# Planned page places, stored transform parts and shifted due times in a one-core FNet and feed-forward kernel

## The chip, the cores and the metric

The kernel runs on one core of a Trainium2 chip. The metric is the device time of one execution in microseconds (us); three runs of the kernel before gave 699.50, 700.13 and 700.16, median 700.13. The engines of the core are named as the profile names them: PE multiplies matrices (PEld is its weight load), DVE is the vector engine, ACT the scalar engine, POOL is GpSimd, and SP only issues DMAs here. Each engine works through its own queue in order; POOL and SP also issue DMAs from theirs.

## The reference

The input `x` has 2048 rows (tokens) of 512. All arrays are float32.

```python
a = jnp.einsum("bsd,ed->bse", x, dft_hid_re)        # x: after layernorm
b = jnp.einsum("bsd,ed->bse", x, dft_hid_im)
y = jnp.einsum("ts,bse->bte", dft_seq_re, a) - jnp.einsum("ts,bse->bte", dft_seq_im, b)

h = x + _A_ref(_layernorm(x, axis=-1), ...)         # _A_ref gives y
h2 = h + W2(silu(W1(_layernorm(h, axis=-1))))       # 512 -> 1792 -> 512
```

So there is a layernorm, a transform along the sequence and along the model dimension of which the real part is kept, a residual sum, a second layernorm and a feed-forward block with SiLU.

## The kernel before

**Precision.** Every float32 operand is split in a rounded part ("hi", type fp32r, made by ACT) and a remainder ("lo", made by DVE). A product is three matmuls: hi by hi, hi by lo, lo by hi (`three`, L124). The two halves of such a split are put in the order of work by `halves` (L87): ACT a lead of 2.2 us (`GAP_US`) ahead of DVE, and DVE with a lead of `PREP_US` = 8 us ahead of the matmuls in most places.

**Stages.** The sequence transform comes first, over four blocks (`c` is real or imaginary part, `q` is a half of the tokens): `plain(0,0)` multiplies directly; `fast(1,0)`, `fast(0,1)` and `fast(1,1)` use seven products for eight (Strassen's scheme in Winograd's form), for which DVE makes sums of blocks of the matrix (`prep`, L426, with four raw blocks loaded by `load`, L421). After two blocks of one `q` follows `mix(q)` (L486), the transform along the model dimension: four products per half `tau`, with the matrix `hid` loaded and split in hi and lo (`load_hid`, `round_h`) in `tau` = 0 and kept for `tau` = 1, once for each `q`. Then `norm_h(q, tau)` (L534) makes the second layernorm of a quarter of the tokens. The order on PE is plain(0,0), fast(1,0), mix(0), fast(0,1), fast(1,1), mix(1), up(0), down(0), up(1), down(1); `up` (W1 and SiLU) and `down` (W2) use seven products for eight as well, and the first products of `down` are put ahead of the last two of `up`.

**norm_h in steps.** `mean` and `var` each add on DVE and then add over partitions on POOL (`total`, L526, an all-reduce). `row` writes one row of 512 variances to HBM, `gather` reads it back as 128 x 4, `root` and `finish` compute the inverse root on DVE, `finish` also issues its write to HBM, `spread` reads it back to all partitions (tile `r`), `scale` (L577) multiplies on DVE. All these DMAs are in POOL's queue. For `q` = 0 `store` writes the normalized parts to HBM (`nd`), from which `load_hn` reads them later; for `q` = 1 they stay on chip until `up(1)`.

**Weights.** `sums_w1` (L622) makes sums of blocks of W1, splits them and stores hi and lo to HBM (`sd`); `fetch_w1` (L648) reads them back for each `q` and loads the plain blocks too. `make_w2` (L751) does the same for W2 (`wd`, four stores of 512 KB for each of seven groups `p`), and `fetch_w2` reads them. These jobs stand beside other stages, at starts that are written out by hand in L908 and L915.

**Order of the work.** Nothing is issued in the order of the source. Each stage puts its pieces in a list `events` with a due time (L130 to L144). The clock of this list counts matmuls alone, 0.2265 us each, from the first one. By it plain(0,0) ends at 87.0, fast(1,0) at 163.1, mix(0) at 206.6, fast(0,1) at 282.7, fast(1,1) at 358.8, mix(1) at 402.3, and the first part of `down(0)` ends at 497.4. A piece that is to stand ahead of a matmul step has a lead: 18 us for a load (`LOAD_US`), 8 for a split. The list is sorted by due time (L940), and the order in which the pieces then come is the order of each engine's queue. In the profile the first matmul starts at 7.25 us, so due time t is at about t + 8.7 in the span in the first part, and later where PE has been idle meanwhile. These due times are called "planned" below.

**Pages.** All tiles of 4 KB per partition are "pages" out of one pool of 51 (L62, L68). Places go round: the 52nd page takes the place of the first, the 53rd that of the second, and so on. Whoever writes a page first waits until the last reader or writer of the tile that had the place is done.

**up and its copies.** In `up`, `post` (L689) copies bank Y out of PSUM to the pages `cp` and `cq` on ACT (n = 1, 6, 5), DVE adds the other bank to it into the page `g` (n = 2, 5, 4), and ACT applies SiLU in place. Before a `down` that finishes later, `keep_bank` (L817) copies PSUM banks out on ACT; `post123` does so for banks 1, 2 and 3 together after the step with n = 3 of the last group. `sums_g` (L799) and two splits prepare each group for the second part of `down`; they start at `first` = clock - 13 and follow every 5 us (L884). `up(q, lead, ...)` spreads the seven sums and splits of its moving operand (`sums_h`, `round_t`, L712) over `lead` us ahead of it: 62 for q = 0, 70 for q = 1.

Of the kernel before, what the change touches and what calls it, by code (L numbers as in the profile page):

```python
# [7 lines left out]
F32 = mybir.dt.float32  # L8
BF16 = mybir.dt.bfloat16
F32R = mybir.dt.float32r  # L10
# [21 lines left out]
PREP_US = 8.0  # L32
LOAD_US = 18.0
GAP_US = 2.2
ORDERED = (mybir.EngineType.PE, mybir.EngineType.DVE, mybir.EngineType.Activation, mybir.EngineType.Pool)


@with_exitstack
def fnet_ffn_kernel(
# [7 lines left out]
    out: bass.AP,  # L47
):


# [19 lines left out]

# [295 lines left out]
    def fast(c, q):  # L366
# [50 lines left out]
        for jj in range(NJ):  # L417
            key = {n: ("A", c, q, n, jj) for n in (5, 7, 6, 4)}
            B4 = {}

            def load(jj=jj, B4=B4):  # L421
                for k, tau in ((0, 1), (0, 0), (1, 1), (1, 0)):
                    load_seq(c, q, jj, k, tau, ("B", k, tau))
                    B4[k, tau] = raw.pop(("B", k, tau))

            def prep(n, jj=jj, B4=B4, key=key):  # L426
                b11, b12, b21, b22 = (B4[k] for k in ((0, 0), (0, 1), (1, 0), (1, 1)))
                o, a, b = {5: (b11, b12, b11), 7: (b12, b22, b12), 6: (b22, b22, b11), 4: (b21, b22, b21)}[n]
                sub(o, a, b)
                raw[key[n]] = o  # L430

            for n in (5, 7, 6, 4):
# [6 lines left out]
                def post(n=n):  # L439
# [9 lines left out]
                    else:  # L449
# [36 lines left out]
    def mix(q):  # L486
        for tau in range(2):
            for c in range(2):
                for i in range(2):
# [34 lines left out]
    nd = dram.tile([2, 2, P, 2, 512], F32, name="nd")  # L524

# [8 lines left out]
    def norm_h(q, tau, start):  # L534
# [22 lines left out]
        def row():  # L557
            nc.gpsimd.dma_start(token[0], ln.pop("v")[0:1, 1, :])

# [13 lines left out]
        def spread():  # L573
            ln["r"] = page(f"r{q}{tau}")
            nc.gpsimd.dma_start(ln["r"][:, 0, :], token[1].partition_broadcast(P))

        def scale(e):  # L577
            v = ln.pop(e)
            for n in range(2):
                nc.vector.tensor_tensor(v[:, n, :], v[:, n, :], ln["r"][:, 0, :], op=ALU.mult)  # L580
            hn[q, e, tau] = v

        def store():
            for e in range(2):
                nc.gpsimd.dma_start(nd[tau, e], hn.pop((q, e, tau)))
# [11 lines left out]
    def load_hn(k, tau):  # L597
        t = hn[0, k, tau] = page(f"hn{k}{tau}")
        nc.sync.dma_start(t, nd[tau, k])

# [47 lines left out]
    def fetch_w1(q, p):  # L648
        load_w1(("W1", q, p), p, False)
# [4 lines left out]
        W[q, p] = {5: (sh, sl, 0), 6: (sh, sl, 1), 7: (sh, sl, 2), 3: (sh, sl, 3)}  # L654

    def round_w1(q, p):
        r = raw.pop(("W1", q, p))
        ah, al = (page(f"w{n}{q}{p}", F32R, (4, 256)) for n in ("ah", "al"))
        nc.scalar.activation(ah[:, 1:, :], r[:, 1:, :], AF.Copy)
        W[q, p].update({1: (ah, al, 1), 2: (ah, al, 2), 4: (ah, al, 3)})  # L660
        return lambda: rest([(al[:, 1:, :], r[:, 1:, :], ah[:, 1:, :])])

    def up(q, lead, between):

        bank, cp = {}, {}

# [18 lines left out]

        def add(f, tau, src, other):
            nc.vector.tensor_tensor(g[q, f][:, tau, :], src, other, op=ALU.add)  # L687

        def post(n, p):  # L689
            if n == 1:  # L690
                cp[p, 0] = page(f"cp{q}{p}")
                cp[p, 1] = page(f"cq{q}{p}")
                for i in range(2):
                    g[q, 2 * p + i] = page(f"g{q}{p}{i}")
                nc.scalar.activation(cp[p, 0][:, 0, :], bank[p, "Y"], AF.Copy)
            elif n == 2:
                add(2 * p, 0, bank[p, "X"], cp[p, 0][:, 0, :])
            elif n == 6:
                nc.scalar.activation(cp[p, 0][:, 1, :], bank[p, "Y"], AF.Copy)
            elif n == 5:  # L700
                nc.scalar.activation(cp[p, 1][:, 0, :], bank[p, "Y"], AF.Copy)
                add(2 * p + 1, 1, bank[p, "V"], cp[p, 1][:, 0, :])
            elif n == 3:
                silu(2 * p, 1, bank[p, "Y"])
            elif n == 4:
                add(2 * p + 1, 0, bank[p, "V"], cp[p, 0][:, 1, :])
# [12 lines left out]
        for v in order:  # L719
# [5 lines left out]
            if n == 1:  # L725
                before = [(LOAD_US, lambda p=p: fetch_w1(q, p)), *halves(PREP_US, lambda p=p: round_w1(q, p))]
            after = [(0, lambda n=n, p=p: post(n, p))]
# [23 lines left out]
    def make_w2(start, p):  # L751
# [6 lines left out]
        def store():  # L758
            for n, t in enumerate((*kept["U"], *kept["V"])):
                nc.gpsimd.dma_start(wd[p, n], t.bitcast(F32))  # L760
# [14 lines left out]
    def down(q, later):  # L775
# [108 lines left out]
        first = clock[0] - PREP_US - 5  # L884
        for p in range(NP):
# [7 lines left out]
        for n, p in order:  # L893
            before, after = [], []
            if n == 6:
                before.append((LOAD_US, lambda p=p: fetch_w2(p, V, 2)))
            if n == 6 and p in (2, 3) and not later:
# [19 lines left out]
    for k in range(2):  # L917
        for tau in range(2):
            at(clock[0] - 80 + 2 * k + tau, lambda k=k, tau=tau: load_hn(k, tau))
# [17 lines left out]


    traced, last = nc.cur_bb.bb.instructions, {}
    for *_, f in sorted(events, key=lambda v: v[:3]):  # L940
        n = len(traced)
        with ExitStack() as order:
            for ins in last.values():
                order.enter_context(tc.issue_after(ins))
            f()
        for ins in traced[n:]:
            if ins.engine in ORDERED:
                last[ins.engine] = ins

# [33 lines left out]
```

## Time and profile before

| | |
|---|---|
| median of three runs | 700.13 us (699.50 to 700.16) |
| the profiled execution's own time | 696.92 us |
| its span, from the first to the last instruction | 694.8 us |
| PE busy | 680.4 us, 98%, 2965 matmuls (13 of them to warm up) |
| DVE busy | 557.6 us, 80% |
| ACT busy | 337.9 us, 49% |
| POOL busy | 80.0 us, 12% |
| DMA | 170.70 MB, 246 GB/s over the span |
| granted TensorE clock | 0.996 |

A matmul's record is 0.39 us long though a new one starts every 0.23 us, since they overlap; so the busy share of PE says that it seldom has nothing to do, and the loss of time is better read from the distance between starts, or from the number of matmuls in slices of equal length.

### The profile page before, as it was taken

Reading aid. Unit: us, or ns where it says so; the run is one execution under the profiler, and the core shown is the slowest. Engines: PE = TensorE matmul, PEld = TensorE weight load, DVE = VectorE, ACT = ScalarE, POOL = GpSimd, SP = SyncE. Lnnn points to the kernel's source line nnn. Section 1 sums busy time; section 2 is a strip of 40 time slices with the busy share of each in tenths; the row PEclk is TensorE's granted clock in tenths of the full one; section 3 lists DMA queues with packets and bytes.
Section 4 is the critical chain, followed back from the end, with each engine's and each line's share of the span. In section 5 each row is a group of like instructions: output and inputs, shape, how many; then the busy total and the mean of one; then the engine's idle time right before and its main releaser. Section 6 shows DMA issues by size and latency. Waiting matters only on the chain.

```text
span 694.8 us, 8384 instructions
## 1 busy us (share of the span) xinstructions
PE 680.4 (98%) x2965; PEld 555.9 (80%) x2965; DVE 557.6 (80%) x715; ACT 337.9 (49%) x421; POOL 80.0 (12%) x99
## 2 busy tenths in 40 slices
PE   8999999999999999999999999989989999999997
PEld 5788888888888887888888888877868888888885
DVE  6599896997887998998998977848999336449975
ACT  4655785544343533555461425637754354565420
POOL 1021020000035211020010232211000000000000
PEclk9999999999999999999999999999999999999999
DMA  8855879677787576899995454578745646688332
GB/s 316 301 194 183 313 258 412 230 259 231 229 282 253 200 260 200 302 319 391 415 386 173 161 193 148 164 267 336 264 168 189 214 145 242 234 325 304 135 139 91
DMA packets 55993, 170.70 MB, mean 246 GB/s; under 512 B 6288, under 2 KB 13456, under 8 KB 55952
## 3 DMA queue, kind: packets, MB, share of 16 engines
q1 hardware_dynamic: 46320, 136.60, 56.5%
q0 software_dynamic: 9632, 33.58, 12.6%
q8 instruction: 23, 0.38, 0.2%
q14 instruction: 18, 0.15, 0.1%
HBM read 133.44 MB, written 36.72 MB: 245 GB/s over the span
## 4 chain that ended last, share of the span: by engine, by line
PE 79%; DVE 7%; issue 5%; DMA 5%; POOL 2%; ACT 2%; DVEq 0%; POOLq 0%
PE m L127 9%; PE m L128 9%; PE m L126 9%; PE y L126 6%; PE y L128 6%; PE y L127 6%; PE f L126 6%; PE f L128 6%; PE f L127 6%; PE c L126 3%; PE c L127 3%; PE c L128 3%; DMA r<-tk 2%; PE vx L128 2%; PE vx L126 2%
## 5 line engine op out<-in xcount | busy, mean ns | idle before, releaser
L77 ACT ACTIVATE ph<-raw 128x1024 fp32r<-128x1024 f32 x98 | 101.7, 1057 | 91.3 <-DVE raw L415 56.5
L81 DVE TENSOR_TENSOR pl<-raw,ph 128x1024 fp32r<-128x1024 f32 x98 | 118.6, 1220 | 16.5 <-ACT ph L77 10.0
L127 PE MATMUL m<-pl,S 128*128 128x512 f32 x192 | 74.9, 390 | 1.6 <-DVE pl L81 1.6
L128 PE MATMUL m<-ph,S 128*128 128x512 f32 x192 | 74.7, 389 | 0.0
L126 PE MATMUL m<-ph,S 128*128 128x512 f32 x192 | 74.7, 389 | 0.0
L126 PE MATMUL f<-gth,wf 128*128 128x512 f32 x168 | 66.1, 393 | 2.7 <-ACT p L819 2.7
L127 PE MATMUL f<-gtl,wf 128*128 128x512 f32 x168 | 66.1, 393 | 0.0
L128 PE MATMUL f<-gth,wf 128*128 128x512 f32 x168 | 66.1, 393 | 0.0
L77 ACT ACTIVATE gth<-g 128x1024 fp32r<-128x1024 f32 x42 | 43.9, 1055 | 41.3 <-DVE g L803 30.9
L415 DVE TENSOR_TENSOR raw<-raw,raw 128x1024 f32<-128x1024 f32 x48 | 60.6, 1263 | 2.1 <-DMA raw<-in_seq 2.1
L126 PE MATMUL m<-ph,X 128*128 128x512 f32 x144 | 56.0, 389 | 0.0
L127 PE MATMUL m<-pl,X 128*128 128x512 f32 x144 | 56.0, 389 | 0.0
L128 PE MATMUL m<-ph,X 128*128 128x512 f32 x144 | 56.0, 389 | 0.0
L81 DVE TENSOR_TENSOR gtl<-g,gth 128x1024 fp32r<-128x1024 f32 x42 | 50.3, 1219 | 0.2 <-DMA wd<-Ul 0.2
L687 DVE TENSOR_TENSOR g<-vx,cp 128x512 f32<-128x512 f32 x28 | 19.3, 689 | 33.0 <-PE vx L128 19.3
L127 PEld LDWEIGHTS m<-pl,S 128*128 128x128 f32 x192 | 36.0, 188 | 9.9 <-DVE pl L81 2.5
L127 PE MATMUL c<-pl,X 128*128 128x512 f32 x112 | 43.5, 390 | 0.0
L126 PE MATMUL c<-ph,X 128*128 128x512 f32 x112 | 43.3, 391 | 0.2 <-ACT X L217 0.2
L128 PE MATMUL c<-ph,X 128*128 128x512 f32 x112 | 43.4, 389 | 0.0
L126 PEld LDWEIGHTS m<-ph,S 128*128 128x128 f32 x192 | 36.1, 188 | 7.5
L128 PEld LDWEIGHTS m<-ph,S 128*128 128x128 f32 x192 | 36.0, 188 | 7.4
L126 PEld LDWEIGHTS f<-gth,wf 128*128 128x128 f32 x168 | 32.0, 190 | 10.1 <-ACT p L819 3.2
(259 smaller groups left out, 1479.8 us busy)
## 6 DMA issues: line engine op xcount, KB each, us to landing
raw<-in_seq SPq DMA_DIRECT2D x98, 512.0 KB, 5.7
wf<-wd SPq DMA_DIRECT2D x56, 512.0 KB, 5.4
sf<-sd SPq DMA_DIRECT2D x28, 512.0 KB, 6.1
w<-in_ffn SPq DMA_DIRECT2D x28, 256.0 KB, 4.5
hid<-in_hid SPq DMA_DIRECT2D x8, 512.0 KB, 6.9
c<-cd SPq DMA_DIRECT2D x8, 512.0 KB, 5.7
h<-in_xT SPq DMA_DIRECT2D x8, 512.0 KB, 5.1
hd<-h POOLq DMA_DIRECT2D x8, 512.0 KB, 4.0
```

The lines of the kernel that those rows point to most:

```text
L77: nc.scalar.activation(hi, src, AF.Copy, scale=sign)
L81: nc.vector.tensor_tensor(lo, src, hi, op=ALU.subtract)
L126: nc.tensor.matmul(acc, wh, mh, start=first, stop=False, skip_group_check=on)
L127: nc.tensor.matmul(acc, wh, ml, start=False, stop=False, skip_group_check=on)
L128: nc.tensor.matmul(acc, wl, mh, start=False, stop=last, skip_group_check=on)
L415: nc.vector.tensor_tensor(o, a, b, op=ALU.subtract)
L687: nc.vector.tensor_tensor(g[q, f][:, tau, :], src, other, op=ALU.add)
```

## The change

- **Pages.** The pool has 51 places with a name each instead of a round. The whole event list is run once ahead of time with stand-ins (`Stub`) that only note, in order, which page each operation uses and at which planned time. `Plan.places` then gives each new page, among the places whose former tile has had all its uses in that order, the one that by the plan has been free for longest; a use counts as over 4 us after its planned time for a matmul, 10 us for a DMA and 2 us for others.
- **The transform's split parts.** In `mix(0)` hi and lo of `hid` are also stored to HBM (`store_hid`, eight DMAs of 512 KB in POOL's queue); in `mix(1)` eight DMAs of 512 KB in SP's queue (`fetch_hid`, lead 13) take the place of four loads and four splits.
- **Second layernorm.** `norm_h(0,1)` starts 57 us after the end of `mix(0)` instead of 6. Its steps have other offsets, for q = 1 `root` and what follows are some 6 us (`scale` 12) later. `spread` writes into the page `v`, and `r` is gone. Both `q` go through HBM (`nd`), and `up` loads them 18 us ahead of its splits.
- **up and down.** The lead of `up(1)` is 24 instead of 70. `cp` and `cq` are gone: ACT copies into the page `g`, and DVE adds in place. `keep_bank` of banks 1 and 2 comes one step (6 matmuls) earlier, and `sums_g` starts 4 us earlier. Stored weights are fetched with a lead of 13 instead of 18.
- **Weights' sums.** Other starts for `sums_w1` and `make_w2`; among them the groups p = 2, 3, 4 of `make_w2` go from planned 291, 311, 331 (in `fast(1,1)`) to 369, 395, 411 (in `mix(1)` and the start of `up(0)`).
- **fast.** The four raw blocks are not loaded together, but two for n = 5, one for n = 7 and one for n = 4, each 18 us ahead of its step.

```diff
+FETCH_US = 13.0
+FREE_US = {None: 2.0, "matmul": 4.0, "dma_start": 10.0}
...
+class Plan:
+    def __init__(self):
+        self.now, self.uses, self.taken, self.last = 0.0, 0, [], []
+    def page(self, name, dt=F32, shape=(2, 512)):
+        self.taken.append(self.uses)
+        self.last.append((self.uses, self.now))
+        return Stub(self, len(self.taken) - 1)
+    def used(self, page, op):
+        self.uses += 1
+        self.last[page] = self.uses, self.now + FREE_US.get(op, FREE_US[None])
+    def places(self):
+        free = [(-1, -1000.0 + n) for n in range(PAGES)]
+        for taken, last in zip(self.taken, self.last):
+            n = min((n for n in range(PAGES) if free[n][0] <= taken), key=lambda n: free[n][1])
+            free[n] = last
+            yield n
...
-    pages = ctx.enter_context(tc.tile_pool(name="pages", bufs=PAGES))
+    pages = ctx.enter_context(tc.tile_pool(name="pages", bufs=1))
...
-        return pages.tile([P, *shape], dt, tag="pg", name=name)
+        return pages.tile([P, *shape], dt, tag=f"pg{next(places)}", name=name)
...
-            def load(jj=jj, B4=B4):
-                for k, tau in ((0, 1), (0, 0), (1, 1), (1, 0)):
+            def load(n, jj=jj, B4=B4):
+                for k, tau in {5: ((0, 1), (0, 0)), 7: ((1, 1),), 4: ((1, 0),)}[n]:
...
-                step(12, mm, before + [(LOAD_US, load)] * (n == 5), [(0, post)] if jj == NJ - 1 and n in (6, 4) else ())
+                step(12, mm, before + [(LOAD_US, lambda n=n, load=load: load(n))] * (n != 6), [(0, post)] if jj == NJ - 1 and n in (6, 4) else ())
...
+    hs = dram.tile([2, 2, 2, P, 2, 512], F32, name="hs")
+    def store_hid(c, i):
+        for n, t in enumerate(H[c, i]):
+            nc.gpsimd.dma_start(hs[c, i, n], t.bitcast(F32))
+    def fetch_hid(c, i):
+        t = [page(f"H{c}{i}{n}") for n in range(2)]
+        for n in range(2):
+            nc.sync.dma_start(t[n], hs[c, i, n])
+        H[c, i] = [v.bitcast(F32R) for v in t]
...
-                    if tau == 0:
-                        before = [(LOAD_US, lambda c=c, i=i: load_hid(c, i)), *halves(PREP_US, round_h)] + before
+                    if tau == 0 and q == 0:
+                        before = [(LOAD_US, lambda c=c, i=i: load_hid(c, i)), *halves(PREP_US, round_h),
+                                  (PREP_US - 4, lambda c=c, i=i: store_hid(c, i))] + before
+                    elif tau == 0:
+                        before.append((FETCH_US, lambda c=c, i=i: fetch_hid(c, i)))
...
-            norm_h(q, tau, clock[0] + 2 + 4 * tau)
+            norm_h(q, tau, clock[0] + (57 if q == 0 and tau else 2 + 4 * tau))
...
-            ln["r"] = page(f"r{q}{tau}")
-            nc.gpsimd.dma_start(ln["r"][:, 0, :], token[1].partition_broadcast(P))
+            nc.gpsimd.dma_start(ln["v"][:, 0, :], token[1].partition_broadcast(P))
...
-        for d, f in ((0, mean), (7, lambda: center(0)), (9, lambda: center(1)),
-                     (10, lambda: square(0)), (12, lambda: square(1)), (15, var), (21, row), (24.5, gather),
-                     (30, root), (32.5, finish), (36, spread), (43, lambda: scale(0)), (45, lambda: scale(1))):
+        late = 6 * q
+        for d, f in ((0, mean), (8, lambda: center(0)), (10, lambda: center(1)),
+                     (11, lambda: square(0)), (13, lambda: square(1)), (16, var), (22, row), (25.5, gather),
+                     (31 + late, root), (33.5 + late, finish), (36.5 + late, spread),
+                     (45 + 2 * late, lambda: scale(0)), (47 + 2 * late, lambda: scale(1))):
             at(start + d, f)
-        if q == 0:
-            at(start + 47, store)
+        at(start + 49 + 2 * late, store)
...
             if n == 1:
-                cp[p, 0] = page(f"cp{q}{p}")
-                cp[p, 1] = page(f"cq{q}{p}")
                 for i in range(2):
                     g[q, 2 * p + i] = page(f"g{q}{p}{i}")
-                nc.scalar.activation(cp[p, 0][:, 0, :], bank[p, "Y"], AF.Copy)
+                copy(2 * p, 0, bank[p, "Y"])
             elif n == 2:
-                add(2 * p, 0, bank[p, "X"], cp[p, 0][:, 0, :])
+                add(2 * p, 0, bank[p, "X"])
...
+        for n, (k, tau) in enumerate(((0, 0), (1, 0), (1, 1), (0, 1))):
+            at(clock[0] - lead - LOAD_US + n, lambda k=k, tau=tau: load_hn(q, k, tau))
...
             if later:
-                return [keep_bank(n) for n in (1, 2, 3)]
+                return keep_bank(3)
...
-                before = [(LOAD_US, lambda p=p: fetch_w2(p, U, 0)), *halves(PREP_US + 1, lambda p=p: round_one(p)),
+                before = [(FETCH_US, lambda p=p: fetch_w2(p, U, 0)), *halves(PREP_US + 1, lambda p=p: round_one(p)),
...
+                if p == NP - 1 and later:
+                    after = [(0, lambda n=n: keep_bank(n)) for n in (1, 2)]
...
-        first = clock[0] - PREP_US - 5
+        first = clock[0] - PREP_US - 9
...
-    for p, t in enumerate((-24, -12, -5, 30, 61, 68, 88)):
+    for p, t in enumerate((-24, -12, 5, 30, 57, 88, 98)):
         sums_w1(clock[0] + t, p)
...
-    for p, t in enumerate((-378, -358, -111, -91, -71, 28, 46)):
+    for p, t in enumerate((-381, -365, -33, -7, 9, 27, 43)):
         make_w2(clock[0] + t, p)
...
-    up(1, 70, lambda: next(second[1]))
+    up(1, 24, lambda: next(second[1]))
```

More of the change, by code (lines that the diff above doesn't have):

```diff
@@ L33, with __init__, __getattr__, __getitem__ @@
 LOAD_US = 18.0
+FETCH_US = 13.0
 GAP_US = 2.2
+FREE_US = {None: 2.0, "matmul": 4.0, "dma_start": 10.0}
 ORDERED = (mybir.EngineType.PE, mybir.EngineType.DVE, mybir.EngineType.Activation, mybir.EngineType.Pool)
+class Stub:
+    shape = (P, 1)
+    def __init__(self, plan, page=None, op=None):
+        self._plan, self._page, self._op = plan, page, op
+    def __getattr__(self, name):
+        return Stub(self._plan, self._page, name)
+    def __getitem__(self, _):
+        return self
+    def __call__(self, *args, **kwargs):
+        for v in (*args, *kwargs.values()):
+            if isinstance(v, Stub) and v._page is not None:
+                self._plan.used(v._page, self._op)
+        return self
+class Plan:
[14 more added lines that the diff above has]
+            yield n
 @with_exitstack
@@ L66, in fnet_ffn_kernel, with program @@
     dram = ctx.enter_context(tc.tile_pool(name="dram", bufs=1, space=bass.MemoryType.DRAM))
-    def page(name, dt=F32, shape=(2, 512)):
-        return pages.tile([P, *shape], dt, tag="pg", name=name)
+    plan = Plan()
+    stub = Stub(plan)
+    for plan.now, *_, f in program(stub, plan.page, stub, stub, stub, stub, x, xT, seq, hid, ffn, out):
+        f()
+    places = plan.places()
+    def page(name, dt=F32, shape=(2, 512)):
+        return pages.tile([P, *shape], dt, tag=f"pg{next(places)}", name=name)
+    events = program(nc, page, keep, small, psum, dram, x, xT, seq, hid, ffn, out)
+    traced, last = nc.cur_bb.bb.instructions, {}
+    for *_, f in events:
+        n = len(traced)
+        with ExitStack() as order:
+            for ins in last.values():
+                order.enter_context(tc.issue_after(ins))
+            f()
+        for ins in traced[n:]:
+            if ins.engine in ORDERED:
+                last[ins.engine] = ins
+def program(nc, page, keep, small, psum, dram, x, xT, seq, hid, ffn, out):
     def banks(name):
@@ L426, in prep @@
             def prep(n, jj=jj, B4=B4, key=key):
-                b11, b12, b21, b22 = (B4[k] for k in ((0, 0), (0, 1), (1, 0), (1, 1)))
+                b11, b12, b21, b22 = (B4.get(k) for k in ((0, 0), (0, 1), (1, 0), (1, 1)))
                 o, a, b = {5: (b11, b12, b11), 7: (b12, b22, b12), 6: (b22, b22, b11), 4: (b21, b22, b21)}[n]
@@ L520, in mix @@
                     step(24, mm, before, after)
-            norm_h(q, tau, clock[0] + 2 + 4 * tau)
+            norm_h(q, tau, clock[0] + (57 if q == 0 and tau else 2 + 4 * tau))
     hn = {}
-    nd = dram.tile([2, 2, P, 2, 512], F32, name="nd")
+    nd = [dram.tile([2, 2, P, 2, 512], F32, name=f"nd{q}") for q in range(2)]
     def total(a, b, name):
@@ L557, in row @@
         def row():
-            nc.gpsimd.dma_start(token[0], ln.pop("v")[0:1, 1, :])
+            nc.gpsimd.dma_start(token[0], ln["v"][0:1, 1, :])
         def gather():
@@ L584, in store, with load_hn @@
             for e in range(2):
[L585 to L589 removed]
+                nc.gpsimd.dma_start(nd[q][tau, e], hn.pop((q, e, tau)))
+        late = 6 * q
[3 more added lines that the diff above has]
+                     (45 + 2 * late, lambda: scale(0)), (47 + 2 * late, lambda: scale(1))):
             at(start + d, f)
[L591 to L592 removed]
+        at(start + 49 + 2 * late, store)
     T, W, g = {}, {}, {}
[L597 to L599 removed]
+    def load_hn(q, k, tau):
+        t = hn[q, k, tau] = page(f"hn{q}{k}{tau}")
+        nc.sync.dma_start(t, nd[q][tau, k])
     def sums_h(q, n):
@@ L659, in round_w1 @@
         nc.scalar.activation(ah[:, 1:, :], r[:, 1:, :], AF.Copy)
-        W[q, p].update({1: (ah, al, 1), 2: (ah, al, 2), 4: (ah, al, 3)})
+        W.setdefault((q, p), {}).update({1: (ah, al, 1), 2: (ah, al, 2), 4: (ah, al, 3)})
         return lambda: rest([(al[:, 1:, :], r[:, 1:, :], ah[:, 1:, :])])
     def up(q, lead, between):
-        bank, cp = {}, {}
+        bank = {}
         def mul(n, p, first, on):
@@ L684, in silu, with copy, add @@
             nc.scalar.activation(g[q, f][:, tau, :], src, AF.Silu)
-        def add(f, tau, src, other):
-            nc.vector.tensor_tensor(g[q, f][:, tau, :], src, other, op=ALU.add)
+        def copy(f, tau, src):
+            nc.scalar.activation(g[q, f][:, tau, :], src, AF.Copy)
+        def add(f, tau, src):
+            nc.vector.tensor_tensor(g[q, f][:, tau, :], src, g[q, f][:, tau, :], op=ALU.add)
         def post(n, p):
             if n == 1:
-                cp[p, 0] = page(f"cp{q}{p}")
-                cp[p, 1] = page(f"cq{q}{p}")
                 for i in range(2):
                     g[q, 2 * p + i] = page(f"g{q}{p}{i}")
-                nc.scalar.activation(cp[p, 0][:, 0, :], bank[p, "Y"], AF.Copy)
+                copy(2 * p, 0, bank[p, "Y"])
             elif n == 2:
-                add(2 * p, 0, bank[p, "X"], cp[p, 0][:, 0, :])
+                add(2 * p, 0, bank[p, "X"])
             elif n == 6:
-                nc.scalar.activation(cp[p, 0][:, 1, :], bank[p, "Y"], AF.Copy)
+                copy(2 * p + 1, 0, bank[p, "Y"])
             elif n == 5:
-                nc.scalar.activation(cp[p, 1][:, 0, :], bank[p, "Y"], AF.Copy)
-                add(2 * p + 1, 1, bank[p, "V"], cp[p, 1][:, 0, :])
+                copy(2 * p + 1, 1, bank[p, "Y"])
+                add(2 * p + 1, 1, bank[p, "V"])
             elif n == 3:
@@ L705, in post @@
             elif n == 4:
-                add(2 * p + 1, 0, bank[p, "V"], cp[p, 0][:, 1, :])
+                add(2 * p + 1, 0, bank[p, "V"])
         def round_t(n):
@@ L725, in up @@
             if n == 1:
-                before = [(LOAD_US, lambda p=p: fetch_w1(q, p)), *halves(PREP_US, lambda p=p: round_w1(q, p))]
+                before = [(LOAD_US, lambda p=p: load_w1(("W1", q, p), p, False)), (FETCH_US, lambda p=p: fetch_w1(q, p)),
+                          *halves(PREP_US, lambda p=p: round_w1(q, p))]
             after = [(0, lambda n=n, p=p: post(n, p))]
@@ L758, in store @@
         def store():
-            for n, t in enumerate((*kept["U"], *kept["V"])):
+            for n, t in enumerate((*kept.pop("U"), *kept.pop("V"))):
                 nc.gpsimd.dma_start(wd[p, n], t.bitcast(F32))
@@ L895, in down @@
             if n == 6:
-                before.append((LOAD_US, lambda p=p: fetch_w2(p, V, 2)))
+                before.append((FETCH_US, lambda p=p: fetch_w2(p, V, 2)))
             if n == 6 and p in (2, 3) and not later:
@@ L914, in fnet_ffn_kernel @@
     mix(1)
-    for p, t in enumerate((-378, -358, -111, -91, -71, 28, 46)):
+    for p, t in enumerate((-381, -365, -33, -7, 9, 27, 43)):
         make_w2(clock[0] + t, p)
-    for k in range(2):
-        for tau in range(2):
-            at(clock[0] - 80 + 2 * k + tau, lambda k=k, tau=tau: load_hn(k, tau))
     second = down(0, True), down(1, False)
@@ L936, in fnet_ffn_kernel @@
         nc.tensor.matmul(idle[:, 0, :], warm[:, :P], warm, start=True, stop=True)
[L939 to L948, printed above, removed]
+    return sorted(events, key=lambda v: v[:3])
 def kernel(A_x, A_dft_seq_re, A_dft_seq_im, A_dft_hid_re, A_dft_hid_im, B_x, B_w1, B_w2):
```

5 lines of the change are left out of this document (2 added, 3 removed).

## The prediction

> **What bounds the kernel now.** I read the page first, then a table of slices of 20 us, then the order in time on PE at the slices that stand out, and last the order in time on DVE, ACT and POOL just ahead of those places, with the chain that ended last.
>
> ```profile
> span 694.8 us, 8384 instructions
> PE 680.4 (98%) x2965; PEld 555.9 (80%) x2965; DVE 557.6 (80%) x715; ACT 337.9 (49%) x421; POOL 80.0 (12%) x99
> ```
>
> PE is the bound, and its 2965 matmuls are the same before and after. So the question is only how much time passes in which PE could run and doesn't. In the order in time, 54 matmuls lie between these two rows:
>
> ```profile
> 257.77 0.39 PE L126 MATMUL m<-ph,X 128*128 128x512 f32 x1
> 270.01 0.39 PE L126 MATMUL m<-ph,S 128*128 128x512 f32 x1
> ```
>
> That is 12.24 / 54 = 0.2267 us each when nothing is missing. A full slice of 20 us then shows 89 or 90 matmuls (those over its edges count too). The slices that matter (span, then busy time and count of PE, PEld, DVE, ACT, POOL, then granted clock, DMA share and GB/s):
>
> ```profile
> 160.00:180.00 20.00, 20.00 (x90) 16.56 (x89) 16.48 (x17) 7.62 (x8) 1.59 (x3) 1.00 0.87 257
> 180.00:200.00 20.00, 20.00 (x90) 16.54 (x89) 15.88 (x18) 6.49 (x7) 4.63 (x5) 1.00 0.76 262
> 260.00:280.00 20.00, 18.37 (x80) 14.54 (x79) 18.18 (x25) 7.43 (x7) 2.69 (x5) 1.00 0.69 199
> 340.00:360.00 20.00, 20.00 (x90) 16.56 (x89) 19.91 (x22) 10.49 (x11) 2.13 (x4) 1.00 1.03 411
> 380.00:400.00 20.00, 20.00 (x90) 16.57 (x89) 18.75 (x16) 8.88 (x9) 4.49 (x3) 1.00 0.46 170
> 400.00:420.00 20.00, 20.00 (x90) 16.56 (x89) 13.16 (x16) 6.36 (x8) 5.80 (x5) 1.00 0.59 203
> 420.00:440.00 20.00, 19.83 (x88) 16.09 (x87) 17.54 (x31) 11.72 (x19) 7.46 (x5) 1.00 0.51 160
> 460.00:480.00 20.00, 17.22 (x72) 12.81 (x71) 12.97 (x20) 11.04 (x18) 2.68 (x5) 1.00 0.90 329
> 500.00:520.00 20.00, 17.26 (x72) 13.91 (x71) 19.69 (x24) 10.05 (x10) 0.00 (x0) 0.95 0.50 179
> 520.00:540.00 20.00, 20.00 (x86) 16.43 (x86) 19.73 (x23) 8.38 (x8) 0.00 (x0) 0.96 0.58 197
> 540.00:560.00 20.00, 20.00 (x90) 16.53 (x90) 4.04 (x4) 7.12 (x8) 0.00 (x0) 1.00 0.63 226
> ```
>
> Missing against 90 are 10, 2, 18, and 18 + 4 matmuls: 2.3, 0.4, 4.1 and 5.0 us, 11.8 in all. By neighbouring starts the last is nearer 4.6, since edges count; I use 2.2 + 0.4 + 4.0 + 4.6 = **11.2 us** of removable loss. Nothing else in the span loses more than some tenths after the start-up.
>
> **What is late in each place.** DVE, POOL, then ACT and PE, in order of time:
>
> ```profile
> 271.81 1.29 DVE L580 TENSOR_TENSOR hr<-hr,r 128x512 f32<-128x512 f32 x2 [1.65 <-DMA r<-tk]
> 419.39 0.69 DVE L687 TENSOR_TENSOR g<-vx,cp 128x512 f32<-128x512 f32 x1 [4.29 <-ACT wah L659]
> 464.62 0.96 DVE L223 TENSOR_TENSOR wal<-w,wah 128x768 fp32r<-128x768 f32 x1 [2.50 <-DMA wd<-Ul]
> 467.43 0.69 DVE L687 TENSOR_TENSOR g<-vx,cp 128x512 f32<-128x512 f32 x1 [1.86 <-DMA wd<-Vh]
> 469.95 2.50 DVE L580 TENSOR_TENSOR hr<-hr,r 128x512 f32<-128x512 f32 x4 [1.82 <-DMA r<-tk]
> ...
> 492.99 0.68 DVE L803 TENSOR_TENSOR g<-g 128x512 f32<-128x512 f32 x1
> 504.29 1.22 DVE L81 TENSOR_TENSOR T3l<-hr,T3h 128x1024 fp32r<-128x1024 f32 x1
> 510.48 1.22 DVE L606 TENSOR_TENSOR hr<-hr,hr 128x1024 f32<-128x1024 f32 x1
> 512.75 0.69 DVE L803 TENSOR_TENSOR g<-g 128x512 f32<-128x512 f32 x1
> ```
>
> ```profile
> 456.30 0.54 POOL L571 DMA_DIRECT2D tk<-rs  x1 [12.16 <-DVE rs L122]
> 456.83 0.54 POOL L760 DMA_DIRECT2D wd<-Uh  x1
> 461.19 0.56 POOL L575 DMA_DIRECT2D r<-tk  x1 [2.25 <-PE y L128]
> ```
>
> ```profile
> 515.65 1.06 ACT L77 ACTIVATE gth<-g 128x1024 fp32r<-128x1024 f32 x1 [0.31 <-DVE g L803]
> 516.61 2.83 ACT L819 ACTIVATE p<-f 128x1024 f32<-128x1024 f32 x3
> 514.54 0.39 PE L128 MATMUL f<-gth,wf 128*128 128x512 f32 x1
> 517.67 0.53 PE L126 MATMUL f<-gth,wf 128*128 128x512 f32 x1 [2.74 <-ACT p L819]
> 518.01 0.62 PE L127 MATMUL f<-gtl,wf 128*128 128x512 f32 x1
> 520.99 0.60 PE L128 MATMUL f<-gth,wf 128*128 128x512 f32 x1
> ```
>
> At 272, `scale` of norm_h(0,1) stands at the head of DVE's queue and waits for the broadcast `r`, in the part of fast(0,1) where DVE is nearly full; splits behind it come late. At 462 to 475, two DVE writes wait until stores of W2's parts have landed whose page they get: those stores stood 12 us in POOL's queue behind a DMA that waited for `finish`. Then `scale` waits for `r` again, whose own issue had waited 2.25 us for a page. At 514, PE waits for ACT to copy bank 1 out; ACT was free to do so earlier, but the copies stand behind the split of `sums_g` for p = 3. The starts from 518.01 to 520.99, 7 steps, are 0.426 us apart, so this idle time also costs 7 x 0.2 = 1.4 us at half speed.
>
> **The change part by part.** (1) *norm_h(0,1) 51 us later.* DVE in fast(0,1) loses its `root`, `finish` and `scale` from the full part, and the wait. The 2.2 us at 272 go. What is late next is the same chain at planned 297 to 310, in fast(1,1). The chain of waits has it so far:
>
> ```profile
> 262.51 5.08 DMA tk<-rs
> 268.21 3.57 DMA r<-tk
> 461.19 8.73 DMA r<-tk
> ```
>
> From 262.51 to 271.78 it takes 9.3 us; `scale` is now due 45 - 33.5 = 11.5 us after `finish` instead of 10.5, so it waits for nothing at that price, and the splits due behind it have 8 - 1.22 = 6.8 us of cover. Bounds: 0, and by a slower DMA the 4.9 us of the last rival. I take 0: the W2 stores that filled this stretch leave it.
>
> (2) *make_w2 and the order in POOL.* Group p = 5 now stores at planned 440.3, ahead of `finish` (447.8) instead of behind it, so its pages come free some 16 us earlier; `scale` of norm_h(1,1) is due 11.5 + 6 = 17.5 us after `finish`, against the 13.6 us from the issue at 456.30 to the landing at 469.9, of which 2.25 were the page wait of `r`, gone with `r`. The 4.0 us at 462 to 475 go. Cover is not large: some 3 us for what `finish` itself takes and for a slower DMA, and behind `scale` the copies of `up` have about 2.7 us (two steps of 6 matmuls).
>
> (3) *keep_bank and sums_g earlier, lead 24.* From 492.99 to 512.75 DVE needed 19.8 us for three rounds planned at 15; the T split and its sum in between (2 x 1.22) move to the stretch that had DVE at 4.04 of 20. With 4 us earlier on top, the split for p = 3 ends some 6 us earlier, about 3 us before the end of the first part, and two of the copies are due one step (1.36 us) before it. The 4.6 us at 514 go, half speed included.
>
> (4) *The cost: two more groups of make_w2 in mix(1) and up(0).* One group on DVE is four sums and two remainders:
>
> ```profile
> L746 DVE TENSOR_TENSOR v<-u,v 128x256 f32<-128x256 f32 x3 | 1.3, 421 | 0.0
> L81 DVE TENSOR_TENSOR pl<-raw,ph 128x1024 fp32r<-128x1024 f32 x98 | 118.6, 1220 | 16.5 <-ACT ph L77 10.0
> ```
>
> 4 x 0.42 + 2 x 1.22 = 4.1 us; p = 3 and 4 add 8.2 to 400 to 440, where DVE has 40 - 13.16 - 17.54 = 9.3 us idle. It fits on average; where it is bunched, ACT's SiLU waits for DVE's add, the copies behind it come late, and PE with them: that is the 0.4 us at 432 now. The `root` and `finish` of norm_h(1,0), about 2.6 us, leave the bunch (6 us later). Bounds 0 and 4.1 (one whole group late); I take 1.0, nearer to nothing because of that relief. The 0.4 at 432 go into this figure.
>
> (5) *HBM for H.* Four splits fewer in mix(1) (DVE 4 x 1.22, ACT about as much): hidden, PE is the bound. Eight stores in POOL at 0.54 to issue each: 4.3 us in 22 us where POOL is busy under a quarter. Due 4 us ahead of the four steps from planned 163.1 on, they bring 4 MB into 168 to 190 of the span, or 190 GB/s on top of 257 to 262: 450, over the 411 moved in 340 to 360. The excess of 40 GB/s over 22 us is 0.9 MB, loads 2 us late, under a cover of 6.8: nothing. In mix(1) eight loads replace four, in a stretch at 170 to 203 GB/s: nothing.
>
> The Trainium skill ("DMA: Bandwidth & Descriptors", section "Where 436 GB/s comes from") puts HBM traffic of a core at about 358 GB/s. By that the excess in mix(0) would be 92 GB/s over 22 us, 2.0 MB, and an estimate of 5.6 us of delay, near the end of that cover, so the sum would keep nothing but the chance of a stall there would grow. The trace moved 411 in the row above, so I go by the trace.
>
> (6) *Pages, cp and cq, loads in fast.* The plan can only bring a place earlier if its times are right. SP waits and PE seldom does, so this is cover: 0. Splitting the four loads leaves 18 - 12.4 = 5.6 us from issue to the sum against this row:
>
> ```profile
> raw<-in_seq SPq DMA_DIRECT2D x98, 512.0 KB, 5.7
> hn<-nd SPq DMA_DIRECT2D x4, 512.0 KB, 11.1
> ```
>
> Level by plan; a sum that waits 1 to 2 us has 12.4 - 1.22 - 1.06 - 1.22 = 8.9 us of cover. Bounds 0 and 2; I take 0.
>
> **Sum.** 2.2 + 0.4 + 4.0 + 4.6 - 1.0 = 10.2 us off the profiled span: 694.8 to 684.6. The profiled execution took 696.92, 3.2 less than the median of the runs; I take the difference from the median: 700.13 - 10.2 = **689.9**.
>
> **Rivals.** *A second bunch.* Both added groups of make_w2 come whole onto PE, 8.2 us: 700.13 - 11.2 + 8.2 = 697.1. For it: DVE at 38.9 of 40 there. Against: DVE idles 4 us before 419 and bunches are shorter than a group.
>
> *It doesn't do what it says.* The losses come from queue order and the new dates only move them: DVE's waits for `r` and ACT's copies behind splits recur elsewhere, about 700. For it: the small cover in (2). Against: each of the three has its own remedy.
>
> *Slower.* In fast(1,1) `scale` of norm_h(0,1) waits at the head of DVE for two DMAs in POOL's queue, in the stretch that now shows the DMA engines full. With L us each, PE stands for 2L + 1 - 11.5 - 6.8. At the 11.1 of `hn<-nd`, the slowest load in the table, it is 4.9 us, some 694 to 695; it decides from L = 15: 12.7, and 1.4 for half speed, so 703. Against: the longest broadcast took 8.73, and 6 MB of W2 stores leave the stretch.
>
> **Numbers.** Forecast 0.60, own range 688.5 to 694; second bunch, or a part of it and of the DMA wait (694 to 698.7), 0.15; no effect 0.08; slower 0.17. A difference under 0.2%, 1.4 us, can't be told from none: faster 0.75, same 0.08, slower 0.17. The range goes from 687.5 (nothing lost but start-up) to 699.5, with the first two and half of the third.
>
> **What would show it.** (1) 89 or 90 matmuls in every slice from 260 to 290, no wait of `hr` for `r`. (2) No DVE wait for a store of `wd` or for `r` between 440 and 475. (3) Copies `p<-f` of banks 1 and 2 ahead of the last product with n = 3, clock 1.00 from 500 to 540. (4) DVE near 19 of 20 around 420, and at most 4 matmuls missing. (5) Loads in mix(0) on time. It is wrong if a new idle place over 3 us shows on PE, above all in fast(1,1) or up(0).

## The result and the profile after

The changed kernel takes 695.86 us (median of 20 runs, 692.36 to 698.26), the kernel before in 20 runs 697.95 (695.54 to 700.75; the three known before lay above this median). The ratio of the two over these runs is 0.9966 (95% interval 0.9951 to 0.9981): by it the change is **2.4 us faster, where 10.2 were forecast**; the medians differ by 2.1. All ratios leave out one execution of e8, which took 979.72 us at a granted clock of 0.654. First the page after, then the slices of 20 us that answer to those of before, with three that aren't in its table (columns as in the prediction).

```profile
span 690.6 us, 8385 instructions
PE 677.4 (98%) x2965; PEld 554.8 (80%) x2965; DVE 553.4 (80%) x711; ACT 335.0 (49%) x417; POOL 84.7 (12%) x111
```

```profile
40.00:60.00 20.00, 19.44 (x86) 15.79 (x86) 18.56 (x36) 13.27 (x19) 5.52 (x7) 1.00 0.64 230
260.00:280.00 20.00, 20.00 (x90) 16.57 (x89) 19.97 (x17) 7.64 (x8) 4.07 (x1) 1.00 0.43 143
320.00:340.00 20.00, 19.54 (x86) 15.72 (x85) 16.44 (x17) 7.34 (x8) 1.08 (x2) 1.00 0.84 292
420.00:440.00 20.00, 19.75 (x87) 16.02 (x87) 18.93 (x35) 12.09 (x19) 6.09 (x7) 1.00 0.74 257
460.00:480.00 20.00, 20.00 (x90) 16.54 (x89) 13.61 (x24) 14.22 (x23) 3.74 (x7) 1.00 1.01 369
500.00:520.00 20.00, 19.78 (x88) 16.05 (x87) 19.59 (x25) 11.12 (x11) 0.00 (x0) 1.00 0.93 336
640.00:660.00 20.00, 17.01 (x75) 13.41 (x74) 19.62 (x24) 7.48 (x8) 0.00 (x0) 1.00 0.63 214
```

The three losses that the prediction counted are gone or small (90, 90 and 88 matmuls at 260, 460 and 500). But 15 matmuls, 3.4 us, are missing at 640 to 660, where the prediction expected nothing. From neighbouring starts on PE, in us beyond 0.2267 a matmul:

| place in the span | before | after |
|---|---|---|
| start of the first matmul, and the start-up after it | 7.25 + 1.5 | 7.88 + 1.6 |
| 59, plain(0,0) | 0 | 0.8 |
| 272 to 278, fast(0,1) | 2.2 | 0 |
| 329 to 332, fast(1,1) | 0 | 0.8 |
| 427 to 449, up(0) | 0.4 | 0.7 |
| 462 to 475, up(0) | 4.0 | 0 |
| 514 to 521, down(0) | 4.6 | 0.5 |
| 645 to 652, down(1) | 0.2 | 3.5 |

The sum is 4.4 us less, the spans differ by 4.2. So 10.3 us were won at three places, and 5.9 of them were lost again at others. What stands at 645, on DVE, ACT and PE of the changed kernel:

```profile
645.41 1.42 DVE L888 TENSOR_TENSOR g<-g,g 128x512 f32<-128x512 f32 x2
648.61 1.22 DVE L900 TENSOR_TENSOR p<-f,r 128x1024 f32<-128x1024 f32 x1
646.19 1.06 ACT L144 ACTIVATE gth<-g 128x1024 fp32r<-128x1024 f32 x1 [2.54 <-DVE g L888]
647.16 1.00 ACT L904 ACTIVATE p<-f 128x1024 f32<-128x1024 f32 x1
644.84 0.39 PE L195 MATMUL f<-gth,wf 128*128 128x512 f32 x1
648.22 0.50 PE L193 MATMUL f<-gth,wf 128*128 128x512 f32 x1 [2.99 <-ACT p L904]
```

It is the picture of 514 before, in the other `down`: bank 1's copy (L904) stands in ACT's queue behind a split that waits for `sums_g` (L888). `first` = clock - 17 holds for both `down`, the earlier copies only for the first. For one group p, `sums_g` and the splits behind it take DVE 5.05 us (called a round below). In down(1) of the kernel before, four rounds stand ahead of DVE's add L815 (L900 here); in the changed kernel five, the fifth from 644.69 on, the row at 645.41 being part of it.

### The profile page after: what moved, and what is told of

Same layout as the page of the kernel before. It is cut to its first block, busy times and chain, and to the rows that moved or that the text cites. A ratio compares the mean times of both kernels' runs of the same rounds, so it can differ in the third digit from the quotient of the medians.

```text
span 690.6 us, 8385 instructions
## 1 busy us (share of the span) xinstructions
PE 677.4 (98%) x2965; PEld 554.8 (80%) x2965; DVE 553.4 (80%) x711; ACT 335.0 (49%) x417; POOL 84.7 (12%) x111
## 4 chain that ended last, share of the span: by engine, by line
PE 76%; DVE 12%; DMA 5%; issue 3%; ACT 3%; POOL 0%; SPq 0%; DVEq 0%; ACTq 0%; POOLq 0%
PE m L194 9%; PE m L195 9%; PE m L193 9%; PE y L193 8%; PE y L194 8%; PE y L195 8%; PE f L193 4%; PE f L195 4%; PE f L194 4%; DVE gtl L148 3%; PE vx L193 3%; PE vx L195 3%; PE vx L194 3%; PE c L194 2%; PE c L195 2%
## 5 line engine op out<-in xcount | busy, mean ns | idle before, releaser
L771 DVE TENSOR_TENSOR g<-vx,g 128x512 f32<-128x512 f32 x42 | 28.8, 688 | 48.3 <-PE vx L195 22.2
```

The costliest lines, as they stand in the source:

```text
L771: nc.vector.tensor_tensor(g[q, f][:, tau, :], src, g[q, f][:, tau, :], op=ALU.add)
```

## The experiments

All ratios are to the kernel before, run on the same chip beside each kernel. Line numbers are those of each kernel.

**e1: the changed kernel again.**

> The changed kernel once more, for a second trace. Its first trace (span 690.6 us) was its shortest of 20 executions. Theory 1 (the new loss stands in down(1), where sums_g starts 4 us earlier and the copy of bank 1 in ACT's queue is behind a split): again 3 to 5 us without a matmul around 645, and 0.5 to 4 us around 330, where scale waits for the broadcast in fast(1,1). Theory 2 (the losses are chance of the DMAs, in other places each time): nothing at 645 in this trace, and other places instead. Ratio to the kernel before 0.995 to 0.998.

Ratio 0.9962 (0.9942 to 0.9983), span 690.2. PE's starts at 644.40 and 647.77 are 3.37 us apart, as in the first trace (3.38); at 331 it lost 0.4, at 59 0.8. In both traces the new losses stand in the same places.

**e2: sums_g of down(1) back.**

```diff
-        first = clock[0] - PREP_US - 9
+        first = clock[0] - PREP_US - (9 if later else 5)
```

> The changed kernel with sums_g of down(1) alone back at clock - 13; down(0) keeps clock - 17. Theory 1: the idle place around 645 falls from 3.4 us to at most 0.3, as in the kernel before at 652; span 3 us less than the changed kernel's in the same call, ratio 0.991 to 0.994. Theory 2: no change beyond 1 us.

Ratio **0.9904** (0.9870 to 0.9938), 689.38 us: 4 us better than the changed kernel. Two slices of e2:

```profile
280.00:300.00 20.00, 18.55 (x82) 15.02 (x82) 19.90 (x18) 11.15 (x11) 7.46 (x4) 1.00 0.54 200
640.00:660.00 20.00, 20.00 (x90) 16.57 (x89) 19.69 (x24) 8.37 (x9) 0.00 (x0) 1.00 0.69 256
```

The loss at 645 is gone: four rounds stand ahead of DVE's add again, which starts at 646.41 instead of 648.61. The span of this one execution is 689.9, since at 294 to 305 PE lost 2.6 us that the first trace didn't show, and some of the first matmuls ran at half speed (granted clock 0.50 for 3.41 us, from 9.28 on). Single spans vary by this much here, so sums go by the ratios, places by the traces.

The 2.6 us seem to hang on one DMA. `scale` of norm_h(0,0) waited 3.50 us on DVE for its broadcast and started at 249.04, in the first trace 1.07 us and at 244.80; the order in DVE's queue is the same there, and DVE, which is full, is still 3.9 us later at the add that fast(1,1) waits for (294.82 against 290.89). With norm_h(0,1) at 57 us, the traces in which this `scale` starts by 246.1 (changed kernel, e1, e7) show no loss at 294 to 305, and those in which it starts at 247.6 or later (e2, e3, e5, e8, e9, e10, e11) all lose 2.2 us or more. No run changed the landing alone.

**e3: only the copy earlier in down(1).** Bank 1 is copied after the step with n = 1 and 2 of the last group, and `post123` leaves its copy out.

```diff
-                if p == NP - 1 and later:
-                    after = [(0, lambda n=n: keep_bank(n)) for n in (1, 2)]
+                if p == NP - 1:
+                    after = [(0, lambda n=n: keep_bank(n)) for n in ((1, 2) if later else (1,))]
```

> The changed kernel with the copy of bank 1 in down(1) one step earlier, as down(0) has it; sums_g as changed. If the order in ACT's queue is the cause alone, the 3.4 us at 645 go (span 3 us less). If DVE's backlog is the cause, the wait only moves on by one product: PE then waits for DVE's add that reads bank 2 (it ended at 649.8 in the changed kernel's trace), the loss stays at 3 to 3.4 us, span within 1 us of the changed kernel's. I expect the second.

Ratio 0.9970 (0.9944 to 0.9996). PE and DVE of e3:

```profile
648.69 0.39 PE L195 MATMUL f<-gth,wf 128*128 128x512 f32 x1
652.37 0.50 PE L193 MATMUL f<-gth,wf 128*128 128x512 f32 x1 [3.29 <-DVE p L900]
651.10 1.22 DVE L900 TENSOR_TENSOR p<-f,r 128x1024 f32<-128x1024 f32 x1
```

The copy came in time, and PE stood one product later, for DVE's add that reads bank 2, behind the same five rounds: 3.5 us, and 5.1 with the half speed that followed in this trace. In down(1) the cause is what DVE, full here, has to do first; ACT's order is only one of its ways.

**e4: the kernel before with the two copies of down(0) earlier**, as the change has them, and nothing else.

> The kernel before with one edit: copies of banks 1 and 2 in down(0) one step earlier. If step 3 of the prediction is right in that ACT's order made the 4.6 us at 514, nearly all of it goes, half speed included: 0.5 us left, span 4 us less, ratio 0.993 to 0.996. If DVE's load there is the cause, as in down(1), 2 us or more stay.

Ratio 0.9940 (0.9921 to 0.9960): 4.2 us, by its estimate more than the whole change (0.9962 on the same chip, e1), though the intervals overlap. ACT of e4:

```profile
511.95 1.92 ACT L819 ACTIVATE p<-f 128x1024 f32<-128x1024 f32 x2
515.78 1.01 ACT L819 ACTIVATE p<-f 128x1024 f32<-128x1024 f32 x1
```

Two copies are done at 513.9 instead of beginning at 516.6; PE lost 0.3 at 516 and 0.4 at 537.

**e10: e2 with the three copies of down(0) together again.**

> e2 with the copies of banks 1, 2 and 3 in down(0) together again after the last product with n = 3; sums_g 4 us earlier and lead 24 stay. Step 3 of the prediction names three remedies for the 4.6 us at 514. If the order of the copies is the one that matters (as e4 says, where it alone left 0.4 us), 2.5 to 5 us come back at 514 to 518, ratio 0.994 to 0.997. If the earlier sums alone would have done, at most 1 us comes back.

Ratio 0.9927 (0.9902 to 0.9952): 1.6 us more than e2 by the estimate, less than expected and with intervals that overlap. The trace is clearer: 4.8 us are lost at 512 to 519, against 0.5 in e2. ACT and PE of e10:

```profile
513.84 1.06 ACT L144 ACTIVATE gth<-g 128x1024 fp32r<-128x1024 f32 x1 [2.57 <-DVE g L888]
514.81 2.83 ACT L904 ACTIVATE p<-f 128x1024 f32<-128x1024 f32 x3
512.46 0.39 PE L195 MATMUL f<-gth,wf 128*128 128x512 f32 x1
515.86 0.80 PE L193 MATMUL f<-gth,wf 128*128 128x512 f32 x1 [3.01 <-ACT p L904]
518.59 0.63 PE L193 MATMUL f<-gth,wf 128*128 128x512 f32 x1
```

With sums 4 us earlier and lead 24, but late copies, the old loss is back: 3.2 us and 7 matmuls at half speed. Earlier sums do nothing for 514: they put one more round ahead of the copies, five for four, so that the copies wait for the split of the next group (p = 4) instead.

**e5: e2 with pages in a round.**

```diff
-    pages = ctx.enter_context(tc.tile_pool(name="pages", bufs=1))
+    pages = ctx.enter_context(tc.tile_pool(name="pages", bufs=PAGES))
-        return pages.tile([P, *shape], dt, tag=f"pg{next(places)}", name=name)
+        return pages.tile([P, *shape], dt, tag="pg", name=name)
```

> The changed kernel with sums_g of down(1) back (as e2, ratio 0.990) and the pages again in a round of 51 places; all due times, copies and stores as changed. Theory 1 (the losses were made by the order of queues, and the plan of places gives only cover): within 1 us of e2, ratio 0.989 to 0.992, no wait of PE over 1 us at 460 to 480. Rival (the places cured the waits of DVE for stores of wd at 462 to 475): 2 to 4 us more there, ratio 0.994 or higher. The first matmul starts at 7.25 again if the other pool has changed the order at the start, at 7.6 to 8.3 if not.

Ratio 0.9965 (0.9946 to 0.9984): 4 us more than e2, against the expectation and with the rival. ACT, then PE, then one slice of e5:

```profile
463.11 0.60 ACT L768 ACTIVATE g<-y 128x512 f32<-128x512 f32 x1 [4.54 <-DMA wd<-Uh]
463.75 0.50 PE L193 MATMUL y<-T5h,sf 128*128 128x512 f32 x1 [2.26 <-ACT g L768]
280.00:300.00 20.00, 18.18 (x74) 14.59 (x73) 19.72 (x17) 10.17 (x10) 7.00 (x4) 0.91 0.38 145
```

ACT's copy into a new page `g` waits 4.5 us for a store of W2's parts that still reads from this place, and PE loses 2.4 us. That part of the loss at 462 to 475 was made by places. Of the rest of the 4 us, 1.1 in this trace are half speed behind a stop at 294 (last section), which needn't come in every execution. The first matmul begins at 7.30 again, so the other pool had also changed the order at the start.

**e6: e2 with norm_h(0,1) at 6 us after mix(0).**

> e2 with the start of norm_h(0,1) back at 6 us after mix(0). The prediction's step 1: the 2.2 us at 272 to 278 come back, and nothing else changes, ratio 0.993. Rival, from the trace of e2 (PE lost 0.7 at 253, 1.7 at 294 and 0.9 at 304, where the moved all-reduce, centering and mean now stand in the full part of DVE): those 3 us go at the same time, so the sum is 0 to 1 us, ratio 0.989 to 0.992. I hold with the rival.

Ratio 0.9913 (0.9890 to 0.9936), not apart from e2. PE lost 1.7 us at 252 and nothing of note at 272 or 290 to 305.

**e7: e2 with the order at the start and two starts of make_w2 as before.** The first remainders become a piece of their own behind the inverse root.

```diff
-        at(-98, lambda: rest(begin_x(keys[0], 0)))
+        at(-98, lambda: early("a", lambda: begin_x(keys[0], 0)))
+        at(-97.5, lambda: rest(late.pop("a")))
...
-    for p, t in enumerate((-381, -365, -33, -7, 9, 27, 43)):
+    for p, t in enumerate((-378, -358, -33, -7, 9, 27, 43)):
```

> e2 with two repairs: the remainder pl in the first piece at the start stands behind the inverse root again, and make_w2 for p = 0 and 1 starts at planned 24 and 44 as before. Theory: the first matmul starts at 7.25 again (7.6 to 8.3 in the traces of the changed order), 0.4 to 1.0 us less, and the 0.8 us at 59 go; ratio 0.987 to 0.989. If the start only waits for the first DMA, nothing changes there and the sum is 0.8.

Ratio 0.9894 (0.9873 to 0.9916); not apart from e2 by the times. In the trace the first matmul starts at 7.36, and the 0.8 at 59 are gone. DVE at the start, first in the kernel before, then in the changed kernel:

```profile
6.41 0.16 DVE L183 SCALAR_TENSOR_TENSOR rs<-mv,rs 128x1 f32<-128x1 f32 x1
6.49 0.69 DVE L223 TENSOR_TENSOR pl<-raw,ph 128x512 fp32r<-128x512 f32 x1
```

```profile
5.09 0.69 DVE L290 TENSOR_TENSOR pl<-raw,ph 128x512 fp32r<-128x512 f32 x1
7.03 0.16 DVE L250 SCALAR_TENSOR_TENSOR rs<-mv,rs 128x1 f32<-128x1 f32 x1
```

With a pool of other places the remainder `pl` comes in the middle of the inverse root instead of behind it, and the factors for the first split are ready 0.6 us later, of which the first load made 0.1. e5 starts at 7.30 and still loses 1.1 at 59, so the loss at 59 belongs to the starts of make_w2 and not to this order. In e7's mix(0), PE stood at two matmuls for 1.9 us in all; ACT of e7 ahead of it:

```profile
187.61 1.06 ACT L144 ACTIVATE H11h<-hid 128x1024 fp32r<-128x1024 f32 x1 [6.80 <-DMA hid<-in_hid]
```

Here a load beside the eight stores came late, which the prediction's step 5 held to be covered. That the stores made it late wasn't tried apart.

**e8: e2 with hid loaded and split in mix(1) again**, nothing of it stored.

> e2 with hid loaded and split in mix(1) again, nothing of it stored: POOL has 8 DMAs of 512 KB less, DVE four splits (4.9 us) more in mix(1). The prediction's step 5 (hidden): within 1 us of e2. Rival: the eight stores make the DMAs of norm_h(0,0) late (DVE waits 3.5 us for the broadcast at 249 in e2), which feeds the losses at 253, 294 and 304; without them 2 to 3 us less, ratio 0.987. Other rival: the splits come back into a full DVE in mix(1), 1 to 3 us more.

Ratio 0.9950 (0.9929 to 0.9970): 3.2 us more than e2, slightly over the other rival's range; the intervals touch, but in the trace the loss at 430 to 436 is 4.2 us, against 0.4 in e2. DVE and PE of e8:

```profile
428.20 2.46 DVE L828 TENSOR_TENSOR v<-u,v 128x256 f32<-128x256 f32 x1
432.45 0.79 PE L193 MATMUL vx<-T7h,sf 128*128 128x512 f32 x1 [2.49 <-DVE g L768]
433.04 0.63 PE L194 MATMUL vx<-T7l,sf 128*128 128x512 f32 x1
```

The splits fill DVE in mix(1), its backlog reaches the start of up(0), and PE waits 2.5 us for an add there, then runs 6 matmuls at half speed. The losses at 253, 294 and 304 stayed, so the stores aren't their cause.

**e9: e2 with make_w2 for p = 2, 3, 4 back in fast(1,1).**

> e2 (ratio 0.990) with make_w2 for p = 2, 3, 4 back in fast(1,1), planned 291, 311, 331. Step 4 of the prediction (two groups in a bunched up(0) cost PE about 1 us, now 0.4 at 430 and 0.2 at 451): these go, and nothing else changes: 0.6 us less. Rival: DVE in fast(1,1) gets 12 us more, where norm_h(0,1) now has its chain (PE lost 1.7 at 294 and 0.9 at 304 in e2): 2 to 4 us more there, ratio 0.993 to 0.996. I hold with the rival, since both jobs then stand in the same stretch.

Ratio 0.9925 (0.9905 to 0.9945), 0.0021 above e2 with intervals that overlap. The losses at 430 and 451 go, and five others of 0.2 to 1.2 us, 3.7 in all, come between 335 and 369. One slice of e9:

```profile
360.00:380.00 20.00, 18.89 (x83) 14.91 (x82) 19.88 (x18) 10.10 (x11) 1.74 (x4) 1.00 1.03 416
```

**e11 and e12: the repairs together**: e7, hid loaded 8 us earlier in mix(0), `scale` of norm_h(0,0) 4 us later; e12 also has norm_h(0,1) at 6 us, both scales later.

> All repairs on the changed kernel: sums_g of down(1) back, the order at the start, W2's first two starts, hid loaded 8 us earlier in mix(0) (it landed late at 179 and 187 in e7, PE lost 1.9 at 189), scale of norm_h(0,0) 4 us later (DVE waited up to 3.5 us for its broadcast at 249). Theory (each of these waits has its own place and price): span 685 to 686, ratio 0.985 to 0.987. Rival (the DMAs move the losses to another place): like e7, 0.989.

> The same, with norm_h(0,1) at 6 us after mix(0) instead of 57 and both scales of q = 0 4 us later. From e6 (2 us less at 294 to 305, 1.5 at 252 from the wait for the broadcast, which is now due later): ratio 0.984 to 0.987. Rival: the chain in the full part of fast(0,1) makes PE wait again at 272, 2 us more than e11.

Ratios **0.9860** (0.9839 to 0.9880) and **0.9861** (0.9842 to 0.9880), 688.58 and 688.68 us: by the ratios some 9.7 us below the kernel before, and both beat the changed kernel; their intervals overlap e2's. The spans, 687.6 and 687.3, lie above the 685 to 686 that were expected of e11. What e11 still waits for where fast(1,1) begins, at 292 to 303 (2.8 us lost there):

```profile
PE m L193 <- DVE p L510: 1.7, 1, 1.7
PE m L194 <- DVE pl L148: 0.5, 1, 0.5
```

Its `scale`, due 4 us later, starts at 248.15, which is late again. e12 loses nothing there, but 0.9 at 248 and 2.0 at 255 to 268, so some 3 us are lost in these two traces with the chain of norm_h(0,1) in either place (e6 lost 1.7).

## Why the prediction was wrong

**The step that failed is (3), its term "sums_g 4 us earlier".** The prediction counted it as a gain in down(0) and gave it no price in down(1), though the edit stands in the code of both. Measured, it wins nothing in down(0) (e10) and costs 3.3 us at 645, some 4 us by the ratios (0.9962 in e1, 0.9904 in e2, on one chip). The slice of down(1) was not in its table: before, it was at full count with DVE nearly full,

```profile
640.00:660.00 20.00, 20.00 (x89) 16.28 (x88) 19.32 (x23) 7.00 (x7) 0.00 (x0) 1.00 0.45 150
```

so a fifth round put ahead of the add made the add and the copy late. The question what then stands ahead of them in the queues was asked of one `down` only. With the edit undone in down(1), 6.7 us of the 10.2 are there (e2); its trace loses the rest at the start, at 59 and at 294 to 305, places that the sum left out or put at nothing.

- (1) The 2.2 us at 272 went, but not because the layernorm was moved: with it moved back (e6) they stay away, and the sum is the same. What cured them, the places, the page `r` or the steps' other offsets, wasn't tried apart. The wait for the broadcast turned up at 326 as the last rival has it, 3.6 us on DVE, most of it under cover: 0.8 on PE.
- (2) The 4.0 us at 462 to 475 went. The prediction gave all to POOL's order and nothing to the places; e5 shows that 2.4 of them need the places.
- (3) For 514 it was right in the cause and the size, but of its three remedies the copies' order alone (e4) brings 4.2 us.
- (4) 1.0 taken, 0.7 found, and moving three groups (p = 2, 3, 4) back is no gain (e9).
- (5) "Hidden" was wrong: the four splits less are worth 3.2 us net of the stores and loads (e8), because DVE, not PE's own time, decides in the bunch behind mix(1). In most traces nothing was late beside the eight stores; in e7's a load was.
- (6) Pages at 0 was wrong: 4 us by the ratios (e5 to e2), of which the trace places 2.4 in up(0).
- The start was not in the sum: 0.6 us later by an order that changed with the pool, and 0.8 at 59, both gone in e7.

The two mistakes in (5) and (6) hid behind terms that were right in sum: what was put down to POOL's order needed the places, and what was put at 1.0 for the bunch held because H's splits had left. That these two terms came out was luck. Of the rivals the "second bunch" (3.0 us saved) came nearest, with the wrong place. The median of 700.13 that the forecast started from was 2.2 us above that of 20 runs, so 695.86 lies only 6 us from 689.9 though 8 us of the saving are missing by the medians. In the last rival 689.9 + 12.7 + 1.4 is 704, not 703; nothing hangs on it.

The rest of the way from 4.2 us (spans) to 2.4 (ratio) lies in that the profiled execution was the shortest of 20. Half speed is the likely reason. Behind a stop it lasts 3.41 us in each trace here that shows it (before, e3, e5, e8, e10), which takes 0.0025 off the mean clock of such a span. In the 20 runs that clock is 0.992 to 0.998: the five at 0.998, the first trace among them, have spans of 690.6 to 693.7, the six at 0.992 or 0.994 spans of 695.1 to 696.5. In e2 and e4, which have no loss of 3 us, it is 0.996 to 1.000. A stop of 3 us is followed by half speed in some executions (e3, e10) and was not in the first trace; that this makes the rest is argued from the clock, not shown, since only profiled executions tell where the clock was low.

## What to carry to other kernels

When a constant is changed in code that runs twice, price it in each place, with the slices of each; a stage without loss can be one that has just enough slack. A due time moved by 4 us moves whole pieces in the queues: here one round of 5 us. Ahead of an engine that is full, work on another queue only moves a wait (e3): take work or lateness off the full engine. And undo the edits of a large change one by one: here two that were priced at nothing brought 3 and 4 us, and one that was counted as a gain cost 4.

## What was not expected of the hardware

Half speed follows stops shorter than the one of the kernel before (3.13 us at 514.54), and not always longer ones. PE of e5:

```profile
293.67 0.39 PE L195 MATMUL m<-ph,X 128*128 128x512 f32 x1
295.88 0.61 PE L193 MATMUL m<-ph,X 128*128 128x512 f32 x1 [1.82 <-DVE p L509]
298.85 0.63 PE L194 MATMUL m<-pl,X 128*128 128x512 f32 x1
```

The first two starts are 2.21 us apart, and the 7 steps from 295.88 to 298.85 are 0.424 us each (clock 0.91 in the slice quoted); in e8 a stop of 2.87 us is followed by the same; but in the changed kernel one of 3.38 us at 644.84 by none. The half speed itself has one length in these traces: the granted clock is 0.50 for 3.41 us each time, from 0.2 us ahead of the first matmul after the stop (e8) to 1.3 us behind it (e3). The Trainium skill ("TensorE: Matmul & The Clock Gate", section "What's actually happening") gives an idle window of about 3.4 us that runs freely; the stops of 2.2 and 2.9 us are below it and still went with half speed.
